# Writing the second layer's h into the place of its float16 halves

## The chip, the cores and the metric

One core of a Trainium2 chip runs the whole program. The metric is device time in microseconds (us) of one execution, measured before the change at a median of 731.52 us over three runs (729.27 to 731.77). One further execution was taken with the hardware profiler; that one took 728.16 us, and its trace spans 726.4 us from the first to the last instruction.

## The reference

The program is a top-k attention followed by two feed-forward layers. Everything is float32 in and out.

- Attention: 2 batches of 8 heads, 576 tokens, head size 64. Scores are q times k transposed over the root of 64; in each row only the 32 largest scores stay, then a softmax over them and the product with v.
- The result, as 1152 tokens by 512, goes through layer 1: `h = x @ w_in` (512 by 2048), `g = max(0.01 h, h)`, `g @ w_out` (2048 by 512).
- Then layer 2, with weights of its own: `h = x @ w_in`, `g = h * tanh(log(1 + exp(min(h, 20))))`, `g @ w_out`.

The change touches only how `g` of layer 2 is kept in memory while it is computed, and in what tile `g` of both layers lies.

## The kernel before, in words

The tokens are cut into nine tiles of 128 (t = 0 to 8). Attention runs in 72 slots, one per tile and head. Each feed-forward product keeps the accuracy of float32 by splitting both factors into a float16 "high" and a float16 "low" half and adding three float16 matmuls.

A feed-forward layer of a tile is four **steps**, one for each 512 of the 2048 columns of `h`. A step has two parts on TensorE:

- `product_in` (L634): 48 matmuls of 128x128 into one PSUM tile `ph`. `ph` has two places (pool `ps_m`), which it shares with other users of the tag "m".
- `product_out` (L648): 12 matmuls of 512 columns, which read the halves `gh` and `gl` of the step and add into `y` of the tile (`ps_y`, one place for both layers).

Between them the step makes `gh` and `gl` out of `ph`. In layer 1 that is `leaky` (L661): two ScalarE activations and one subtraction on GpSimd. In layer 2 it is `mish` (L669), a chain over four engines: ScalarE writes `hs` (the scaled h, L672) and `mc` (exp, L674) from `ph`; GpSimd clamps `mc` (L675); ScalarE squares, takes a logarithm and an exponential, all in place on `mc` (L676 to L678); VectorE multiplies by `hs` (L679); GpSimd makes `gh` and `gl` (L681, L682), for the last tile of layer 2 VectorE (`TF`, L820).

Memory is given out by tags, each with a fixed number of places; a new tile waits until the last reader of the place's former tile is done. Tag "t" (`TB = 3` places of 128x512 float32) serves `hs`, `mc`, the `lk` of `leaky`, and `o`, the output of a tile on its way to memory (L719). Tags "gh" and "gl" (`GB = 3` places each, 128x512 float16) serve the halves. They are asked for at the end of `mish` (L680), after its whole chain, and at the start of `leaky` (L663).

The function `step` (L797) emits the work: `first` of one step, that is `product_in` and the chain, and then, once more than `LAG = 3` steps are under way, `second`, that is `product_out`, of the step three before it. The layers alternate by tiles: four steps of layer 1 of tile t, then four of layer 2 of tile t-1; the last four are layer 2 of tile 8. During attention a slot emits one or two steps; after the last slot the rest of the steps follow by themselves.

Instructions are not issued in the order of the program. A planner simulates the engines when the kernel is built. It gives every instruction a priority (`at`, L837; a step gets one that is five slots later than its slot's attention) and, for each engine, picks the ready instruction of highest priority; an instruction that needs a place not yet free is not ready. What comes out is a fixed order for each engine, and on the chip each engine follows it and waits at semaphores.

Of the kernel before, what the change touches and what calls it, by code (L numbers as in the profile page):

```python
# [8 lines left out]
F16 = mybir.dt.float16  # L9
BF16 = mybir.dt.bfloat16  # L10
F32 = mybir.dt.float32
# [7 lines left out]
def topk_attention_moe_moe2_kernel(  # L19
# [18 lines left out]
    P = 128  # L38
# [25 lines left out]
    tmp = ctx.enter_context(tc.tile_pool(name="tmp", bufs=1))  # L64
    xtp = ctx.enter_context(tc.tile_pool(name="xtp", bufs=1))
    gp = ctx.enter_context(tc.tile_pool(name="gp", bufs=1))
# [589 lines left out]
    GB = 3  # L656

    def halves():
        return [gp.tile([P, 512], F16, tag=c, name=c, bufs=GB) for c in ("gh", "gl")]

    def leaky(ph, g, beside):  # L661
        t = tmp.tile([P, 512], F32, tag="t", name="lk", bufs=TB)
        gh, gl = halves()  # L663
        nc.scalar.activation(gh, ph, AF.Prelu, scale=fac[0][:, g:g + 1], alpha=0.01)
        nc.scalar.activation(t, ph, AF.Prelu, scale=fac[0][:, g:g + 1], alpha=0.01)  # L665
        beside.tensor_tensor(out=gl, in0=t, in1=gh, op=ALU.subtract)  # L666
        return gh, gl

    def mish(ph, g, iv, beside):  # L669

        hs = tmp.tile([P, 512], F32, tag="t", name="hs", bufs=TB)
        nc.scalar.activation(hs, ph, AF.Identity, scale=fac[1][:, g:g + 1])  # L672
        c = tmp.tile([P, 512], F32, tag="t", name="mc", bufs=TB)
        nc.scalar.activation(c, ph, AF.Exp, scale=iv[:, g:g + 1])  # L674
        nc.gpsimd.tensor_scalar(out=c, in0=c, scalar1=E20, scalar2=0.0, op0=ALU.min, op1=ALU.max)  # L675
        nc.scalar.activation(c, c, AF.Square, bias=1.0)  # L676
        nc.scalar.activation(c, c, AF.Ln, scale=0.5, bias=0.5)
        nc.scalar.activation(c, c, AF.Exp, scale=-1.0)  # L678
        nc.vector.scalar_tensor_tensor(out=c, in0=c, scalar=1.0, in1=hs, op0=ALU.subtract, op1=ALU.mult)  # L679
        gh, gl = halves()  # L680
        beside.tensor_scalar(out=gh, in0=c, scalar1=1.0, scalar2=0.0, op0=ALU.mult, op1=ALU.add)  # L681
        beside.tensor_tensor(out=gl, in0=c, in1=gh, op=ALU.subtract)  # L682
        return gh, gl
# [3 lines left out]
    class Layer:  # L687
# [11 lines left out]
        def first(self, g):  # L699
            ph = product_in(2 * self.l, self.hi, self.lo, g)  # L700
            beside = nc.vector if FG * self.t + g >= TF[self.l] else nc.gpsimd
            self.gs[g] = mish(ph, g, self.iv, beside) if self.l else leaky(ph, g, beside)
# [20 lines left out]
    TB = 3  # L723
# [138 lines left out]
    for i in range(-2, NS):  # L862
# [22 lines left out]
        if i >= 0:  # L885
            t, h = slots[i]
# [15 lines left out]
    n = NS  # L902
# [35 lines left out]
```

## Time and profile before

| | |
|---|---|
| median of three runs | 731.52 us (729.27 to 731.77) |
| the profiled execution | 728.16 us, its span 726.4 us |
| mean granted TensorE clock | 0.950 |
| TensorE busy | 636.1 us, 88% of the span |
| VectorE busy | 550.6 us, 76% |
| ScalarE busy | 547.7 us, 75% |
| GpSimd busy | 457.5 us, 63% |

Busy time is an average over a span with several stages: attention runs to about 617 us, the first `hs` is written at 267.9 us, and after 617 us only steps of the two layers are left. In the rows further down, PE is TensorE (PEld its weight loads), DVE VectorE, ACT ScalarE, POOL GpSimd, and SPq the queue that issues the DMAs. A row of a list of waits names the waiting instruction, what released it, then us in total, how many times, and the longest.

### The profile page before, as it was taken

Reading aid. Unit: us, or ns where it says so; the run is one execution under the profiler, and the core shown is the slowest. Engines: PE = TensorE matmul, PEld = TensorE weight load, DVE = VectorE, ACT = ScalarE, POOL = GpSimd, SP = SyncE. Lnnn points to the kernel's source line nnn. Section 1 sums busy time; section 2 is a strip of 40 time slices with the busy share of each in tenths; the row PEclk is TensorE's granted clock in tenths of the full one; section 3 lists DMA queues with packets and bytes.
Section 4 is the critical chain, followed back from the end, with each engine's and each line's share of the span. In section 5 each row is a group of like instructions: output and inputs, shape, how many; then the busy total and the mean of one; then the engine's idle time right before and its main releaser. Section 6 shows DMA issues by size and latency. Waiting matters only on the chain.

```text
span 726.4 us, 16854 instructions
## 1 busy us (share of the span) xinstructions
PE 636.1 (88%) x6420; PEld 455.5 (63%) x6420; DVE 550.6 (76%) x1199; ACT 547.7 (75%) x1068; POOL 457.5 (63%) x724
## 2 busy tenths in 40 slices
PE   2478788989977998889989999997999999999995
PEld 1254354557666886576667767666677777776772
DVE  3988988997899667798879899989799798120112
ACT  5497688988687888788979896877697788553643
POOL 2969967778965656566757676566567578333230
PEclk9999789998966997999999999999999999999999
DMA  8662373352332102243256223343444343200000
GB/s 290 229 220 84 116 272 121 108 176 75 124 116 74 60 1 54 61 83 74 39 111 113 51 56 72 65 82 61 65 78 71 74 60 55 62 17 16 1 16 29
DMA packets 107217, 64.14 MB, mean 88 GB/s; under 512 B 93696, under 2 KB 97792, under 8 KB 107136
## 3 DMA queue, kind: packets, MB, share of 16 engines
q1 hardware_dynamic: 107136, 63.06, 34.0%
q8 instruction: 50, 0.82, 0.5%
q14 instruction: 31, 0.25, 0.1%
HBM read 41.16 MB, written 2.36 MB: 60 GB/s over the span
## 4 chain that ended last, share of the span: by engine, by line
PE 34%; DVE 17%; ACT 16%; DMA 13%; POOL 13%; issue 7%; SPq 0%; POOLq 0%; ACTq 0%; DVEq 0%
DMA pts<-warena 6%; DVE top L512 6%; POOL warena L158 5%; PE ph L643 4%; PE ph L644 4%; PE ph L645 4%; DVE wk L515 4%; PE y L652 4%; PE y L654 4%; PE y L653 4%; DMA warena<-in_moe_w_in_dram 3%; PE lp L263 2%; ACT wk L537 2%; PE sps L497 2%; POOL warena L570 2%
## 5 line engine op out<-in xcount | busy, mean ns | idle before, releaser
L643 PE MATMUL ph<-xt,warena 128*128 128x128 f16 x1152 | 206.2, 222 | 3.1 <-ACT mc L674 2.4
L644 PE MATMUL ph<-xt,warena 128*128 128x128 f16 x1152 | 205.8, 222 | 0.0
L645 PE MATMUL ph<-xt,warena 128*128 128x128 f16 x1152 | 205.7, 222 | 0.0
L512 DVE MAX8 top<-wk 128x8 f32<-128x576 f32 x216 | 158.4, 751 | 1.2
L644 PEld LDWEIGHTS <-warena 128*128 128x128 f16 x1152 | 114.9, 100 | 8.2 <-issue 3.5
L643 PEld LDWEIGHTS <-warena 128*128 128x128 f16 x1152 | 115.0, 100 | 7.7 <-issue 2.2
L652 PE MATMUL y<-warena,gl 128*128 128x512 f16 x288 | 110.4, 383 | 6.9 <-ACT o L720 2.2
L645 PEld LDWEIGHTS <-warena 128*128 128x128 f16 x1152 | 114.5, 99 | 2.4 <-issue 1.0
L158 POOL TENSOR_TENSOR warena<-warena 128x256 int32<-128x256 int32 x128 | 104.2, 847 | 17.3 <-DVE warena L219 5.2
L654 PE MATMUL y<-warena,gh 128*128 128x512 f16 x288 | 110.2, 383 | 0.0
L653 PE MATMUL y<-warena,gh 128*128 128x512 f16 x288 | 110.0, 382 | 0.0
L515 DVE MATCH_REPLACE8 wk<-top,wk 128x576 f32<-128x576 f32 x144 | 106.9, 742 | 0.0
L537 ACT ACTIVATE wk<-sc,nb,iv 128x576 f32<-128x576 f32 x72 | 62.4, 867 | 20.7 <-POOL nb L530 20.4
L497 PE MATMUL sps<-kst,qst 128*128 128x288 f16 (+1 forms) x320 | 63.3, 306 | 9.7 <-ACT sc L499 7.4
L512 DVE MAX8 top<-sc 128x8 f32<-128x576 f32 x72 | 53.8, 747 | 21.4 <-ACT sc L499 17.7
L679 DVE SCALAR_TENSOR_TENSOR mc<-mc,hs 128x512 f32<-128x512 f32 x36 | 25.5, 708 | 55.3 <-ACT mc L678 55.3
L499 ACT COPY sc<-sps 128x288 f32<-128x288 f32 x144 | 53.7, 397 | 11.9 <-PE sps L497 11.8
L538 ACT ACTIVATE wk<-wk,nb 128x576 f32<-128x576 f32 x72 | 56.0, 777 | 8.5 <-POOL nb L534 7.6
L666 POOL TENSOR_TENSOR gl<-lk,gh 128x512 f16<-128x512 f32 x36 | 42.8, 1191 | 20.8 <-ACT lk L665 19.9
L530 POOL TENSOR_SCALAR nb<-top,iv 128x1 f32<-128x1 f32 x72 | 25.2, 350 | 47.0 <-DVE top L512 40.0
L263 PE MATMUL lp<-warena,diag 128*128 128x512 f32 x80 | 50.8, 722 | 3.1 <-POOL diag L258 1.8
L515 DVE MATCH_REPLACE8 wk<-top,sc 128x576 f32<-128x576 f32 x72 | 53.5, 743 | 0.0
(192 smaller groups left out, 1543.2 us busy)
## 6 DMA issues: line engine op xcount, KB each, us to landing
warena<-in_moe_w_in_dram SPq DMA_DIRECT2D x16, 1024.0 KB, 5.5
warena<-in_moe_w_out_dram SPq DMA_DIRECT2D x11, 1024.0 KB, 5.0
warena<-in_moe_w_out_dram SPq DMA_DIRECT2D x10, 512.0 KB, 3.3
out_dram<-o SPq DMA_DIRECT2D x9, 256.0 KB, 2.2
qr<-in_q_dram SPq DMA_DIRECT2D x8, 256.0 KB, 3.4
rawkv<-in_v_dram SPq DMA_DIRECT2D x8, 256.0 KB, 3.7
rawkr<-in_k_dram SPq DMA_DIRECT2D x6, 256.0 KB, 3.2
rawkv<-in_k_dram SPq DMA_DIRECT2D x2, 256.0 KB, 8.2
```

Source lines behind the costliest of these rows:

```text
L158: nc.gpsimd.tensor_tensor(out=o[:, a:a + PIECE], in0=o[:, a:a + PIECE], in1=x[:, a:a + PIECE], op=ALU.add)
L263: nc.tensor.matmul(lp, lhsT=diag, rhs=raws[c + i], start=True, stop=False)
L497: nc.tensor.matmul(sps[p0:p0 + n, :HS], lhsT=lq[:, c, p0:p0 + n], rhs=rk[:, half * HS:(half + 1) * HS], start=(c == 0), stop=(c == 1))
L512: queued(nc.vector.max(out=top[:, 8 * r:8 * r + 8], in_=src))
L515: queued(nc.vector.match_replace(out=wk, in_to_replace=top[:, 8 * r:8 * r + 8], in_values=src, imm_value=NEG))
L537: nc.scalar.activation(e, sc, AF.Prelu, bias=nb[:, 0:1], scale=iv, alpha=1e30)
L643: nc.tensor.matmul(o, lhsT=wb, rhs=xa, start=(c == 0), stop=False)
L644: nc.tensor.matmul(o, lhsT=wa, rhs=xb, start=False, stop=False)
L645: nc.tensor.matmul(o, lhsT=wa, rhs=xa, start=False, stop=(c == KC - 1))
L652: nc.tensor.matmul(y, lhsT=gb, rhs=whi(j), start=(g == 0 and f == 0), stop=False)
L653: nc.tensor.matmul(y, lhsT=ga, rhs=wlo(j), start=False, stop=False)
L654: nc.tensor.matmul(y, lhsT=ga, rhs=whi(j), start=False, stop=(g == FG - 1 and f == 3))
```

## The change

`gh` and `gl` become the two halves of one tile of 128x2x512 float16, tag "g", with three places. Together they take the same memory as before. In layer 1 nothing else changes. In layer 2 that tile is asked for at the start of `mish`, and `hs`, a 128x512 float32, is written over the whole of it. `hs` is read for the last time by the multiplication on VectorE, whose result goes to `mc`; after it `gh` and `gl` are written over `hs`. Tag "t" no longer holds `hs`.

```diff
     def halves():
-        return [gp.tile([P, 512], F16, tag=c, name=c, bufs=GB) for c in ("gh", "gl")]
+        return gp.tile([P, 2, 512], F16, tag="g", name="gg", bufs=GB)
 
     def leaky(ph, g, beside):
         t = tmp.tile([P, 512], F32, tag="t", name="lk", bufs=TB)
-        gh, gl = halves()
+        both = halves()
+        gh, gl = both[:, 0], both[:, 1]
...
     def mish(ph, g, iv, beside):
 
-        hs = tmp.tile([P, 512], F32, tag="t", name="hs", bufs=TB)
+        both = halves()
+        hs = both.rearrange("p c n -> p (c n)").bitcast(F32)
         nc.scalar.activation(hs, ph, AF.Identity, scale=fac[1][:, g:g + 1])
...
         nc.vector.scalar_tensor_tensor(out=c, in0=c, scalar=1.0, in1=hs, op0=ALU.subtract, op1=ALU.mult)
-        gh, gl = halves()
+        gh, gl = both[:, 0], both[:, 1]
         beside.tensor_scalar(out=gh, in0=c, scalar1=1.0, scalar2=0.0, op0=ALU.mult, op1=ALU.add)
         beside.tensor_tensor(out=gl, in0=c, in1=gh, op=ALU.subtract)
         return gh, gl
```

## Rows read from the trace of the kernel before

**Rows 1.** The page's first part: busy us, share of the span, instructions.
```profile
PE 636.1 (88%) x6420; PEld 455.5 (63%) x6420; DVE 550.6 (76%) x1199; ACT 547.7 (75%) x1068; POOL 457.5 (63%) x724
```
**Rows 2.** Busy time by stage: length, busy us by engine, clock, DMA.
```profile
268.00:290.00 22.00, 18.41 (x159) 15.05 (x157) 14.42 (x32) 20.20 (x49) 12.93 (x20) 0.77 0.19 44
...
310.00:600.00 290.00, 272.87 (x3279) 200.38 (x3278) 260.96 (x577) 236.77 (x494) 189.12 (x342) 0.99 0.39 72
600.00:690.70 90.70, 89.45 (x1045) 65.63 (x1043) 25.40 (x52) 51.17 (x88) 39.17 (x50) 1.00 0.15 29
...
694.50:708.00 13.50, 13.49 (x205) 11.94 (x204) 3.07 (x5) 6.92 (x12) 3.32 (x4) 1.00 0.01 2
708.00:720.10 12.10, 8.17 (x37) 3.41 (x37) 5.14 (x10) 6.30 (x10) 1.78 (x2) 1.00 0.06 22
```
**Rows 3.** What TensorE waited for from 268 to 600 us.
```profile
PE av L583 <- DMA pts<-warena: 9.0, 7, 1.9
...
PE ph L643 <- ACT mc L674: 2.4, 2, 1.4
```
**Rows 4.** What TensorE waited for from 600 us to the end.
```profile
PE y L652 <- ACT o L720: 2.2, 1, 2.2
PE y L652 <- DVE gl L682: 1.7, 1, 1.7
...
PE y L652 <- POOL gl L682: 1.2, 1, 1.2
```
**Rows 5.** What ScalarE waited for from 600 us to the end.
```profile
ACT gh L664 <- PE y L654: 17.8, 5, 4.6
```
**Rows 6.** Groups by line: ScalarE, 268 to 617 us (count, busy us, mean ns, idle before).
```profile
L672 ACT ACTIVATE hs<-ph,fac 128x512 f32<-128x512 f32 x24 | 16.4, 683 | 7.0 <-PE ph L645 6.2 <-POOL gl L682 0.8
```
**Rows 7.** Instructions in time: TensorE near the end (start, us, instruction, [idle before]).
```profile
679.99 0.38 PE L652 MATMUL y<-warena,gl 128*128 128x512 f16 x1
...
682.58 0.22 PE L643 MATMUL ph<-xt,warena 128*128 128x128 f16 x1
...
685.26 0.38 PE L652 MATMUL y<-warena,gl 128*128 128x512 f16 x1
...
691.92 0.39 PE L652 MATMUL y<-warena,gl 128*128 128x512 f16 x1 [1.18 <-POOL gl L682]
...
710.22 0.38 PE L652 MATMUL y<-warena,gl 128*128 128x512 f16 x1 [2.23 <-ACT o L720]
...
720.03 0.39 PE L652 MATMUL y<-warena,gl 128*128 128x512 f16 x1 [1.67 <-DVE gl L682]
```
**Rows 8.** Instructions in time: ScalarE in the attention stage.
```profile
425.98 0.69 ACT L672 ACTIVATE hs<-ph,fac 128x512 f32<-128x512 f32 x1 [0.61 <-PE ph L645]
...
433.58 0.67 ACT L674 ACTIVATE mc<-ph,iv 128x512 f32<-128x512 f32 x1
```
**Rows 9.** Instructions in time: ScalarE near the end.
```profile
680.19 0.69 ACT L672 ACTIVATE hs<-ph,fac 128x512 f32<-128x512 f32 x1 [2.35 <-PE ph L645]
...
683.26 0.69 ACT L674 ACTIVATE mc<-ph,iv 128x512 f32<-128x512 f32 x1
...
704.80 0.69 ACT L672 ACTIVATE hs<-ph,fac 128x512 f32<-128x512 f32 x1 [0.63 <-DVE gl L682]
...
709.48 0.69 ACT L720 ACTIVATE o<-y,ivo 128x512 f32<-128x512 f32 x1 [0.63 <-DVE gl L682]
...
712.28 0.69 ACT L672 ACTIVATE hs<-ph,fac 128x512 f32<-128x512 f32 x1 [0.94 <-DMA out_dram<-o]
...
714.32 0.69 ACT L674 ACTIVATE mc<-ph,iv 128x512 f32<-128x512 f32 x1 [0.83 <-DVE mc L679]
```
**Rows 10.** The tile xt from 689 us on, and its transposing DMA.
```profile
L621 SPq DMA_TRANSPOSE xt<-xp x1: 1232/1232/1232, 690.2 to 690.2; - x1
...
DMA to landing us min/median/max: 3.0/3.0/3.0
```
**Rows 11.** The tile hs: duration in ns (min/median/max), first and last start.
```profile
L679 DVE SCALAR_TENSOR_TENSOR mc<-mc,hs x36: 669/686/1141, 279.4 to 718.0; 128x512 f32<-128x512 f32 x36
```

## The prediction

> **What bounds the kernel now.** I read the page's busy times first: TensorE is the fullest engine at 88% [rows 1]. Then the busy time by stage, which says where the missing 12% lie: from 310 to 600 us TensorE is at 272.87 of 290 us (94%), from 600 to 690.7 at 99%, from 694.5 to 708 at all of it, and only between 708 and 720.1, before the last product, does it fall to 8.17 of 12.1 [rows 2]. So from 310 us on the program ends when TensorE has done its work, and what can be won is its idle time. Third, TensorE's list of waits: between 268 and 600 us most of what it waits for is attention's (9.0 us for the transposed weights `pts` alone), and 2.4 us, in two stalls, are a `product_in` that waits for exp (`mc`, L674) to have read the `ph` it wants to overwrite [rows 3]. After 600 us there are three stalls of layer 2: 2.2 us for `o`, 1.7 and 1.2 us for `gl` [rows 4]. These 7.5 us are what the change can reach.
>
> Why they arise is in ScalarE's order of time. The `hs` at 680.19 us is followed by its exp only at 683.26; near the end `hs` at 704.80, `o` at 709.48, `hs` at 712.28 and exp at 714.32 were each released by the last reader of a tile of tag "t" (VectorE's `gl`, again `gl`, the DMA of `o`, VectorE's multiplication) [rows 9]. With two of three "t" places to a chain, one and a half chains are under way at a time.
>
> **The change, part by part.**
>
> *Instructions.* None is added or taken away, and shapes, types and engines stay: cost 0. In `leaky` the first write is to `gh` as before, and its place comes free with the same `product_out`: 0.
>
> *The new wait.* A place of tag "g" is now held from `hs`, not from `gh`, on. `hs` of a step therefore waits for the `product_out` three steps earlier, which the program puts right behind the step's own `product_in`. One `product_in` takes 685.26 - 682.58 = 2.68 us and one `product_out` 682.58 - 679.99 = 2.59 us [rows 7], so `hs` starts some 2.6 us later in the last stage. Queued behind it on ScalarE are the exp of the same step and whatever attention has there; exp itself now needs only a "t" place and can go first. Waiting for its result is the `product_out` of three steps on, 3 x (2.68 + 2.59) = 15.8 us after the `product_in`. A chain from exp to the release of its `product_out` took 720.03 - 714.32 = 5.7 us for the last step [rows 7, 9], so with 2.6 us of wait and 0.7 us of `hs` it is ready after 9.0 us, 6.8 us early. `leaky` has this wait already: its `gh` waited five times for a `product_out`, up to 4.6 us [rows 5], and no stall of TensorE goes back to it [rows 4]. In attention 24 chains, so 48 steps of both layers, lie in 349 us [rows 6], 7.3 us a step against 5.27 alone; stretched alike, the `product_out` ahead of `hs` is 2.6 x 7.3 / 5.27 = 3.6 us, and `ph` is held for that and two activations of 0.7 us, about 5 us (an estimate). In the stalled case it was held from 425.98 to 434.25 us, 8.3 us [rows 8]. So I take 0; the upper end is the slower rival below.
>
> *The "t" places.* A chain takes one of three instead of two. Stall by stall:
>
> - The 1.18 us before 691.92 us [rows 7]. The chain in question is the one whose exp came 3.07 us behind its `hs` [rows 9]. With a place at hand its `gl` is ready before 690.74 and that `product_out` ends 1.18 us earlier. Next late is the transposed input of the last tile: its DMA is issued at 690.2 us and lands 3.0 us later, 693.2 [rows 10], before the end of that product. Between 0 and 1.18; I take 1.0, since the landing bounds it hardly.
> - The 2.23 us before 710.22. `y` has one place, so the last tile's first `product_out` waits until `o` has read it. `o` waited for a "t" place until 709.48 [rows 9]. Afterwards the three places hold one exp each and the oldest is done before this `y` is. Between 0.8 (two activations of 0.7 us ahead of `o` on ScalarE) and 2.23; I take 2.2.
> - The 1.67 us before 720.03. Without the stall above, the last `product_in` ends at 710.22 - 2.23 = 707.99 and three products of 8.14 / 3 = 2.71 us (710.22 to 718.36) follow, to 716.13. The last `hs` needs the place that the first of them frees, at 710.70. If ScalarE takes exp first, at 708.0, `hs` ends at 711.4 and `gl`, 2.0 us after the multiplication's start (718.0 to 720.03 [rows 7, 11]), at 713.4: the stall is gone. If `hs` goes first, exp starts at 711.3 and `gl` is there at 711.3 + 5.7 = 717.0, which leaves 0.9 us. So 0.8 to 1.67; I take 1.2, between the two orders.
> - The 2.4 us in attention [rows 3]: 0 to 2.4. I take 0.6, since the 9.0 us of waits for `pts` in the same stretch are ahead and behind in one fixed order and take most of what is freed.
>
> A rule of the Trainium skill speaks against the change. The trace shows the multiplication, which reads `mc` and `hs`, at a median of 686 ns with one at 1141 [rows 11]. "SBUF — State Buffer", section "Who interferes with whom", says that a VectorE instruction with two SBUF inputs contends with a GpSimd instruction that reads SBUF, so that one of the two is held. More chains at a time then mean more such meetings; by the trace's worst case, 0.45 us on the last chain, the sum would be 4.5 us instead of 5.0, by the median 5.0.
>
> The sum, made against the profiled execution: 1.0 + 2.2 + 1.2 + 0.6 = **5.0 us**, between 0 + 0.8 + 0.8 + 0 = 1.6 and 7.5. It goes from a span of 726.4 to 721.4 and from 728.16 to 723.2 us. That execution is 3.4 us under the median of 731.52; I carry the difference over: 731.52 - 5.0 = **726.5 us**. A measurement can hardly tell less than 0.5%, 3.7 us, from no change here.
>
> **The rivals.**
>
> - *Slower: the "g" places become the bound.* If the planner puts `hs` late behind attention's work, `ph` is held by `hs` as it is now by exp, and the next `product_in` but one stalls TensorE. Price: the two such stalls of before were 1.2 us each on average [rows 3]; at 8 of the 24 chains in attention [rows 6] that is 9.7 us, against 4.4 us won at the end: 731.5 - 4.4 + 9.7 = 736.8 us. It decides once `ph` is held over some 8 us at every third chain. For it: ScalarE is at 75% and its order is fixed ahead. Against it: the 5 us worked out above, and the rows of `leaky`. A new order in attention that lengthens the waits for `pts` would show in the same place, but would not name `hs`.
> - *No difference: the exp doesn't go ahead.* `hs` stands in front of exp in ScalarE's order, both wait for the `product_out`, and the places gained don't start a chain sooner. Then only `o` comes free (2.2 us), the last stall keeps 0.9 us, and the plan of attention is as good as before: -2.2 - 0.8 = -3.0, so 728.5 us; with attention's waits 1 or 2 us longer, 730. For it: in every pair of before `hs` precedes exp [rows 9].
> - *More: the clock.* From 268 to 290 us the granted clock was 0.77, TensorE moving between its two levels, 1.2 and 2.4 GHz, with 3.6 us of idle time [rows 2]. Here the first chains of layer 2 begin. If they come sooner and fill it, up to 22 x (1 - 0.77) = 5.1 us more are won: 721.4 us. Against it: what it did there was mostly attention's.
>
> **How the numbers follow.** The forecast, 726.5 us, has 0.42; the clock's case 0.08; no difference 0.30; slower 0.20. Faster by over 0.5% is the first two, 0.50; within 0.5% 0.30; slower 0.20. The range reaches down to 720.5, a microsecond below the clock's case, and up to 736, short of the slower rival's 736.8, which leaves out its upper half (0.10) and some 0.05 below. The forecast's own range is 724.0 (all 7.5 us) to 729.9 (1.6 us).
>
> **What would show it.** Right: exp directly behind its `hs` or ahead of it, `hs` released by a `product_out` (L654), `o` at once behind its `y`, no wait for `o` in TensorE's list after 600 us, and at most one for `gl`. Wrong: `product_in` waiting for `hs` (L672) in attention; longer waits for `pts`; the idle time of TensorE between 310 and 600 us above the 17 us of before; or attention ending later, so that TensorE has more left after it.

## The result and the profile after

The changed kernel is faster: against the kernel before, ratio 0.9855 (95% interval 0.9818 to 0.9892), medians 718.97 us (715.21 to 720.49, four runs) and 731.64 us. By the ratio that is 10.6 us on 731.5, where the forecast said 5.0. (The medians lie 12.7 us apart; the gains below go by the ratios.) The profiled execution took 718.89 us, with a span of 717.1 us, 9.3 us less than before.

Busy time by stage of the changed kernel, in stretches like those of [rows 2] (columns: stretch, length, TensorE busy, weight loads, VectorE, ScalarE, GpSimd, granted clock, DMA share, GB/s); the last two lines are two such stretches of the kernel before:

```profile
268.00:310.00 42.00, 35.81 (x249) 23.50 (x247) 24.42 (x59) 33.79 (x80) 22.64 (x33) 0.80 0.18 42
310.00:600.00 290.00, 280.09 (x3416) 208.07 (x3415) 266.84 (x597) 242.33 (x509) 193.28 (x351) 0.99 0.38 74
600.00:717.10 117.10, 111.29 (x1238) 79.20 (x1235) 28.36 (x59) 62.22 (x105) 41.00 (x54) 1.00 0.15 29
...
268.00:310.00 42.00, 35.15 (x304) 26.34 (x302) 29.31 (x71) 35.27 (x83) 23.85 (x38) 0.84 0.25 57
600.00:726.40 126.40, 116.43 (x1309) 83.18 (x1307) 33.61 (x66) 66.93 (x113) 46.04 (x58) 1.00 0.13 27
```

TensorE's idle time (length less busy) from 310 to 600 us fell from 17.1 us [rows 2] to 9.9. From 600 us to the end it fell from 10.0 us (126.4 less 116.4 in the trace before) to 5.8. Those are 7.2 and 4.2 us. Between 268 and 310 us it is 6.2 against 6.9. Ahead of 268 us it is 58.7 against 56.3; the order of the instructions there is the same, so this is scatter between executions. Over the whole span idle fell by 9.6 us, and busy time (636.5) is what it was (636.1 [rows 1]).

TensorE's list of waits from 268 to 600 us, which answers to [rows 3]:

```profile
PE av L583 <- DMA pts<-warena: 2.5, 4, 1.0
...
PE xt L627 <- DVE u L100: 1.3, 2, 1.0
...
PE y L652 <- POOL gg L684: 1.0, 1, 1.0
```

The 9.0 us for `pts` are 2.5 (how much of that is scatter comes up below), and `product_in` no longer waits for exp. The list from 600 us to the end, which answers to [rows 4] (`gg` is the joined tile; VectorE and GpSimd write `gl` at L684):

```profile
PE y L652 <- POOL gg L684: 1.3, 1, 1.3
PE y L652 <- DVE gg L684: 0.9, 1, 0.9
```

The wait for `o` is gone. The two for `gl` are still there, one shorter. ScalarE's list of the same stretch shows the new wait, `hs` (L674) behind a `product_out`, beside that of `leaky` (L665) [rows 5]:

```profile
ACT gg L674 <- PE y L654: 13.0, 10, 2.3
ACT gg L665 <- PE y L654: 12.0, 5, 4.1
```

And the group of the 24 chains in attention, which answers to [rows 6], now with exp (L676) beside it:

```profile
L674 ACT ACTIVATE gg<-ph,fac 128x512 f32<-128x512 f32 x24 | 16.5, 687 | 6.7 <-PE y L654 6.5
L676 ACT ACTIVATE mc<-ph,iv 128x512 f32<-128x512 f32 x24 | 16.5, 686 | 0.0
```

Exp waits for nothing there: it stands right behind its `hs`. Over the 24 chains exp started 4.5 us after its `hs` before, 0.6 us after it now; over the 12 of the last stage 2.0 and 0.6 us (means of the starts in the timelines).

### The profile page after: what moved, and what is told of

Same layout as the page of the kernel before. It is cut to its first block, busy times and chain, and to the rows that moved or that the text cites. A ratio compares the mean times of both kernels' runs of the same rounds, so it can differ in the third digit from the quotient of the medians.

```text
span 717.1 us, 16836 instructions
## 1 busy us (share of the span) xinstructions
PE 636.5 (89%) x6420; PEld 455.2 (63%) x6420; DVE 546.3 (76%) x1199; ACT 544.9 (76%) x1068; POOL 455.4 (64%) x724
## 4 chain that ended last, share of the span: by engine, by line
PE 47%; DVE 16%; ACT 11%; DMA 10%; POOL 9%; issue 5%; SPq 1%; POOLq 0%; ACTq 0%; DVEq 0%
PE ph L645 6%; PE y L653 6%; PE y L652 6%; PE ph L643 6%; PE y L654 6%; PE ph L644 6%; DVE top L512 5%; DVE wk L515 3%; POOL warena L158 3%; PE sps L497 3%; DMA warena<-in_moe_w_in_dram 3%; DMA warena<-in_moe_w_out_dram 3%; DMA pts<-warena 2%; DVE warena L222 1%; ACT warena L260 1%
## 5 line engine op out<-in xcount | busy, mean ns | idle before, releaser
L643 PE MATMUL ph<-xt,warena 128*128 128x128 f16 x1152 | 202.9, 220 | 1.4 <-ACT xt L628 1.0
L644 PE MATMUL ph<-xt,warena 128*128 128x128 f16 x1152 | 202.9, 220 | 1.1 <-DVE u L100 1.1
L645 PE MATMUL ph<-xt,warena 128*128 128x128 f16 x1152 | 202.9, 220 | 0.0
L158 POOL TENSOR_TENSOR warena<-warena 128x256 int32<-128x256 int32 x128 | 105.9, 860 | 18.3 <-DVE warena L219 6.3
L652 PE MATMUL y<-warena,gg 128*128 128x512 f16 x288 | 111.3, 386 | 5.0 <-POOL gg L684 2.3
L653 PE MATMUL y<-warena,gg 128*128 128x512 f16 x288 | 111.4, 387 | 0.0
L654 PE MATMUL y<-warena,gg 128*128 128x512 f16 x288 | 111.3, 387 | 0.0
L537 ACT ACTIVATE wk<-sc,nb,iv 128x576 f32<-128x576 f32 x72 | 62.7, 871 | 32.4 <-POOL nb L530 32.2
L681 DVE SCALAR_TENSOR_TENSOR mc<-mc,gg 128x512 f32<-128x512 f32 x36 | 26.1, 724 | 50.5 <-ACT mc L680 50.5
L538 ACT ACTIVATE wk<-wk,nb 128x576 f32<-128x576 f32 x72 | 56.3, 782 | 4.7 <-POOL nb L534 3.9
L667 POOL TENSOR_TENSOR gg<-lk,gg 128x512 f16<-128x512 f32 x36 | 42.9, 1191 | 23.5 <-ACT lk L666 23.2
L570 POOL TENSOR_TENSOR warena<-wk,warena 128x512 f16<-128x512 f32 x32 | 37.6, 1174 | 26.0 <-ACT warena L569 25.5
```

The source lines that it names most:

```text
L158: nc.gpsimd.tensor_tensor(out=o[:, a:a + PIECE], in0=o[:, a:a + PIECE], in1=x[:, a:a + PIECE], op=ALU.add)
L537: nc.scalar.activation(e, sc, AF.Prelu, bias=nb[:, 0:1], scale=iv, alpha=1e30)
L538: nc.scalar.activation(e, e, AF.Exp, bias=nb[:, 2:3], accum_out=self.sums[:, h:h + 1])
L643: nc.tensor.matmul(o, lhsT=wb, rhs=xa, start=(c == 0), stop=False)
L644: nc.tensor.matmul(o, lhsT=wa, rhs=xb, start=False, stop=False)
L645: nc.tensor.matmul(o, lhsT=wa, rhs=xa, start=False, stop=(c == KC - 1))
```

## The experiments

All ratios are to the kernel before on the same chip. Joining the two halves alone changes nothing: in `e1_tail` below they are joined for all tiles while `hs` stays in tag "t" up to tile 5, and up to 627 us the order on every engine is that of the kernel before, instruction for instruction. So all of the effect comes from where `hs` stands.

**1. The two stages apart.** Do the 10.6 us come from one stage or from two? `e1_tail` applies the change from tile 6 on; `e2_attn`, with `t < 6` in the same place, up to tile 5:

```diff
-        both = halves()
-        hs = both.rearrange("p c n -> p (c n)").bitcast(F32)
+        if t >= 6:
+            both = halves()
+            hs = both.rearrange("p c n -> p (c n)").bitcast(F32)
+        else:
+            hs = tmp.tile([P, 512], F32, tag="t", name="hs", bufs=TB)
...
+        if not (t >= 6):
+            both = halves()
```

> h is written into the halves' place only for tiles 6 to 8 of layer 2, the last twelve chains, after attention; up to there every engine's order is that of the kernel before. If the gain is the sum of two stages (my theory), only the last stage's is here: TensorE idle after 600 us falls from 10.0 us to about 6, idle from 310 to 600 us stays at 17, and the time falls by 4 us, to about 727.5. If the whole gain hung on one stage, the rival, the time would be 721 (the last stage alone) or 731 (attention alone).

> h is written into the halves' place only for tiles 0 to 5 of layer 2, the 24 chains during attention; up to the first chain of tile 6 every engine's order is that of the changed kernel. Sum of two stages: TensorE idle from 310 to 600 us is about 10 us as in the changed kernel, idle after 600 us is about 10 us as before with the wait for o back at some 2 us, and the time falls by 6 to 7 us, to about 725. One stage alone: 721 or 731.

Measured: `e1_tail` 0.9953 (0.9929 to 0.9977), 3.4 us; `e2_attn` 0.9929 (0.9904 to 0.9955), 5.2 us. Together 8.6 of the 10.6 us, within their intervals. Idle time of TensorE from 310 to 600 us: 15.0 us in the first, 10.5 in the second; after 600 us 7.0 and 8.8. So there are two gains; by the medians and the idle times the larger is in attention, though the two intervals overlap, and its 5.2 us are less than the 6 to 7 I expected. `e1_tail` also shows the scatter: up to 627 us its order is that of the kernel before, and yet it has 15.0 us of idle time there and not 17.1. The list of waits after 600 us of `e2_attn` has the three stalls of [rows 4] back:

```profile
PE y L652 <- ACT o L727: 2.2, 1, 2.2
PE y L652 <- DVE gg L689: 1.7, 1, 1.7
PE y L652 <- POOL gg L689: 1.2, 1, 1.2
```

**2. Places or the luck of a new order?** The planner lays out all that follows anew when one thing changes, and the waits for `pts` that shrank have nothing to do with layer 2's places. `b_lswap` is a re-plan without any new place, a mild one: on TensorE the new order starts only at 326 us, not from the first steps on as the expectation has it, and in the traces a matmul moves by 5 places on average, against 19 by the change.

```diff
+        nc.scalar.activation(t, ph, AF.Prelu, scale=fac[0][:, g:g + 1], alpha=0.01)
         nc.scalar.activation(gh, ph, AF.Prelu, scale=fac[0][:, g:g + 1], alpha=0.01)
-        nc.scalar.activation(t, ph, AF.Prelu, scale=fac[0][:, g:g + 1], alpha=0.01)
```

> The kernel before, with the two activations of layer 1's leaky written in the other order; no place and no instruction changes, but the planner's order differs on all engines from the first steps on. If the gain in attention comes from the free places (theory), a new order by itself doesn't give it: TensorE idle from 310 to 600 us stays at 15 to 19 us and the time within 728 to 735. If it was the luck of a new order (rival), the idle time lands anywhere from 8 to 25 us and the time from 722 to 740.

Measured: 1.0008 (0.9986 to 1.003), idle 15.4 us. `a_lswap` is the same edit in the changed kernel:

> The changed kernel with the two activations of leaky written in the other order: a new order on all engines, no other places. Theory (the gain belongs to the places): idle from 310 to 600 us 8 to 12 us, ratio 0.982 to 0.991. Rival (luck of an order): idle 8 to 25 us, ratio 0.975 to 1.01.

Measured: 0.9867 (0.9841 to 0.9893), idle 10.8 us. The gain goes with the change. The two orders without it are nearly the same, so this alone would not rule out luck; the later runs add six more orders, all with a gain.

**3. The swap that was meant as a second re-plan.** `b_swap` is the kernel before with exp written ahead of `hs`:

```diff
         hs = tmp.tile([P, 512], F32, tag="t", name="hs", bufs=TB)
-        nc.scalar.activation(hs, ph, AF.Identity, scale=fac[1][:, g:g + 1])
         c = tmp.tile([P, 512], F32, tag="t", name="mc", bufs=TB)
         nc.scalar.activation(c, ph, AF.Exp, scale=iv[:, g:g + 1])
+        nc.scalar.activation(hs, ph, AF.Identity, scale=fac[1][:, g:g + 1])
```

> The kernel before, with exp written ahead of hs in the chain of layer 2; same places and instructions, a new order from the first chain of layer 2 on. Theory: idle from 310 to 600 us stays at 15 to 19 us, the time within 728 to 735. Rival (luck of a new order): idle 8 to 25 us, time 722 to 740, independent of the other swap's.

Measured: 0.9772 (0.9722 to 0.9823), faster than the changed kernel by its median (the intervals just touch), with idle 9.9 us. Both sides of my expectation missed the time: it is no mere re-plan. A chain still takes the same two places, but exp now takes the first and runs through its powers while `hs`, read only by the multiplication, waits: exp starts 2.7 us ahead of `hs` on average in attention. In ScalarE's list of waits from 268 to 610 us, before (first line) it is exp that waits for a place, which the multiplication frees; in `b_swap` (second line) it is `hs`, and exp waits for its `ph` alone:

```profile
ACT mc L674 <- DVE mc L679: 1.4, 2, 1.2
...
ACT hs L674 <- DVE mc L679: 1.2, 1, 1.2
```

TensorE's list of waits of `b_swap` after 600 us has one row left:

```profile
PE y L652 <- ACT o L720: 0.5, 1, 0.5
```

To see whether that was luck, `b_swap_lswap` adds the edit of 2 to it:

> The kernel before with exp ahead of hs and also leaky's activations in the other order. Alone the first gave 0.977 and the second 1.001. If exp ahead of hs is the cause, 0.972 to 0.985 and idle from 310 to 600 us 8 to 12 us; if the first was a lucky order, 0.985 to 1.005 and idle 12 to 20 us.

Measured: 0.9779 (0.9747 to 0.9811), idle 8.8 us, clear of the changed kernel's interval. Not luck, though this order too is near that of `b_swap` (4 places on average).

**4. Is it the third place?** `a_tb2` is the changed kernel with `TB = 2`.

> The changed kernel with two places of tag t instead of three. Rival (the number of places held by chains makes the gain): two places for exp, lk and o together are fewer than a chain and a half needs, exp is late again, TensorE idle from 310 to 600 us returns to 15 us or more, the wait for o returns, ratio 0.995 to 1.01. Theory (what counts is that exp doesn't stand behind an hs that already holds a place): exp stays within 1.5 us of hs on average, the idle time stays at 8 to 12 us, ratio 0.983 to 0.992, with at most the stall for o back at the end.

Measured: 0.9893 (0.9855 to 0.993). Exp starts 1.1 us after `hs`; idle 12.4 us from 310 to 600 us, a little over what I expected, and 5.8 after 600, and no wait for `o`. So two places for exp, `lk` and `o` give nearly the whole gain that three do. By itself this leaves open that a chain now takes one place of two, not two of three; but `b_swap` has the old three places, two to a chain, and gains as well. What held the kernel before was not how many places there were, but that an `hs` with nothing to do yet took one ahead of the exp that starts the chain.

**5. Both at once.** `a_swap` is the changed kernel with the edit of `b_swap`.

> The changed kernel with exp ahead of hs, so that exp doesn't stand behind an hs that waits for a product_out. Theory: the last stage's idle time falls from 5.8 us to under 4.5 (the last stall of 0.9 us goes, the one before it shrinks), idle from 310 to 600 us stays at 8 to 12 us, ratio 0.975 to 0.984, as good as the other kernel with exp first. If the wait for product_out cost nothing (rival), the ratio is that of the changed kernel, 0.983 to 0.99.

Measured: 0.9898 (0.9851 to 0.9945). The last stage did what was expected (idle 4.1 us, no stall for `gl`), but attention did not: idle 13.2 us, and among its waits 2.2 us for `gl`. My expectation for the ratio failed; the two edits don't add. The rival's range has the ratio, but not its reason: in the last stage the wait for `product_out` did cost something.

**6. Why exp first beats the changed kernel.** Idle time over the whole span is 81.0 us in `b_swap` and 80.6 in the changed kernel, so the 4.9 us between their spans (712.2 and 717.1) lie in TensorE's busy time, 631.2 against 636.5, for the same 6420 matmuls. Of these 5.3 us, 2.0 lie ahead of the matmul at which the two orders part (263.7 and 264.4 us) and are scatter; from there on it is 427.5 against 430.8. The stage whose clock differs most is that of the first four chains. `h1_first_swap` takes `b_swap`'s way for tile 0 and the changed kernel's for the rest, `h2_first_after`, with `t == 0` for `t > 0`, the reverse:

```diff
-        both = halves()
-        hs = both.rearrange("p c n -> p (c n)").bitcast(F32)
-        nc.scalar.activation(hs, ph, AF.Identity, scale=fac[1][:, g:g + 1])
+        if t > 0:
+            both = halves()
+            hs = both.rearrange("p c n -> p (c n)").bitcast(F32)
+            nc.scalar.activation(hs, ph, AF.Identity, scale=fac[1][:, g:g + 1])
         c = tmp.tile([P, 512], F32, tag="t", name="mc", bufs=TB)
         nc.scalar.activation(c, ph, AF.Exp, scale=iv[:, g:g + 1])
+        if not (t > 0):
+            hs = tmp.tile([P, 512], F32, tag="t", name="hs", bufs=TB)
+            nc.scalar.activation(hs, ph, AF.Identity, scale=fac[1][:, g:g + 1])
...
+        if not (t > 0):
+            both = halves()
```

> Exp ahead of hs, with hs in tag t, for tile 0 of layer 2 alone (the first four chains, 268 to about 310 us); all later tiles as in the changed kernel. Theory: exp first beat the changed kernel by what TensorE's clock lost in that first stretch (its idle time is the same, 81 us both); the granted clock from 268 to 310 us is above 0.88, TensorE idle from 310 to 600 us 8 to 13 us and after 600 us about 6 us, ratio 0.975 to 0.983. Rival: exp first wins in all of attention because its hs doesn't hold a place of the halves; then this one is near the changed kernel, 0.984 to 0.99.

> The other way round: tile 0 of layer 2 as in the changed kernel, exp ahead of hs with hs in tag t from tile 1 on. Theory: granted clock from 268 to 310 us about 0.80 as in the changed kernel, idle after 600 us about 4 us, ratio 0.982 to 0.988. Rival: the later tiles make the difference, ratio 0.973 to 0.980 whatever the clock of the first stretch.

Measured: 0.9809 (0.9769 to 0.9848) and 0.9866 (0.9822 to 0.9909), both ratios inside the theory's range, though the interval of the first reaches into its rival's. The stretch from 268 to 310 us, first of `b_swap`, then of `h1_first_swap`, then of `h2_first_after`:

```profile
268.00:310.00 42.00, 34.91 (x275) 22.63 (x274) 30.34 (x73) 35.88 (x85) 23.90 (x37) 0.92 0.21 48
```

```profile
268.00:310.00 42.00, 35.78 (x274) 22.88 (x272) 30.39 (x73) 35.88 (x85) 23.93 (x37) 0.88 0.21 48
```

```profile
268.00:310.00 42.00, 35.67 (x248) 23.23 (x246) 24.50 (x61) 33.90 (x79) 22.64 (x33) 0.80 0.18 42
```

With exp first in those four chains the clock is 0.88 to 0.92 and 274 or 275 matmuls go through in 35 to 36 us; the other way 0.80 and 248. TensorE's busy time from the matmul at which the orders part is 427.4 us in `h1_first_swap` and 426.8 in `b_swap_lswap`, and 430.8 to 433.0 in the four traces with the changed kernel's order there (changed, `e2_attn`, `a_lswap`, `h2_first_after`). So the changed kernel gives back some 3 us. Exp first alone doesn't bring them: `a_swap`, with exp first but `hs` in the halves' place, has 0.89 in this stretch with only 247 matmuls, then 0.97 from 310 to 600 us, and 432.0 us of busy time. The intervals of the two mixed kernels overlap a little, so the sign rests on the medians (714.33 and 719.03 us) and on the clock together.

The idle times side by side (us of TensorE; exp less hs is the mean of 24 chains):

| kernel | exp less hs | idle 310 to 600 | idle after 600 | ratio |
|---|---|---|---|---|
| before | 4.5 | 17.1 | 10.0 | 1 |
| b_lswap | 4.1 | 15.4 | 8.7 | 1.001 |
| e1_tail | 4.4 | 15.0 | 7.0 | 0.995 |
| e2_attn | 0.6 | 10.5 | 8.8 | 0.993 |
| changed | 0.6 | 9.9 | 5.8 | 0.986 |
| a_lswap | 0.6 | 10.8 | 5.8 | 0.987 |
| a_tb2 | 1.1 | 12.4 | 5.8 | 0.989 |
| a_swap | -3.2 | 13.2 | 4.1 | 0.990 |
| h2_first_after | -1.8 | 11.9 | 4.7 | 0.987 |
| h1_first_swap | -0.3 | 10.3 | 5.8 | 0.981 |
| b_swap | -2.7 | 9.9 | 4.0 | 0.977 |
| b_swap_lswap | -3.0 | 8.8 | 4.1 | 0.978 |

The three with exp over 4 us behind `hs` have 15.0 to 17.1 us of idle time in attention, the nine others 8.8 to 13.2. Part of that is scatter (before and `e1_tail` have one order there, and so have changed and `e2_attn`), but the two groups stay apart. `b_swap` and `b_swap_lswap` beat both kernels; exp first, with `hs` left in tag "t", is the better edit.

## Why the prediction was right, and where it was off

**Direction and mechanism: right.** Exp stands right behind `hs`, `hs` is released by a `product_out`, no stall of TensorE names `hs`, and `o` follows its `y` by 1.2 us, in time for the next tile. One sign failed: two waits for `gl` are left, where the prediction allowed one. All of the gain is idle time of TensorE, as the first paragraph of the prediction had it.

**The sum: too small by half, and the time in the range partly by luck.** 10.6 us lie outside the 1.6 to 7.5 us of the forecast's own terms. The time is inside the whole range because that reached down for the clock's case, which did not happen here.

**The new wait, costed at 0: nearly.** `hs` waited ten times for a `product_out` in the last stage, 13.0 us in all, and idle time fell there all the same. But exp stands behind that `hs`. In `a_swap`, where it doesn't, the stage has 4.1 us of idle time and not 5.8, so the wait costs up to 1.7 us; 0.9 of it the prediction had put into its last term.

**The 1.18 us before 691.92: wrong, 1.0 taken, nothing won.** The stall is 1.28 us now. What was late was not the DMA but the chain itself, on VectorE and GpSimd:

```profile
680.44 0.63 ACT L680 ACTIVATE mc<-mc 128x512 f32<-128x512 f32 x1
...
682.12 0.16 DVE L100 TENSOR_SCALAR u<-tot 128x1 int32<-128x1 int32 x1 [5.98 <-PE tot L119]
682.20 0.69 DVE L681 SCALAR_TENSOR_TENSOR mc<-mc,gg 128x512 f32<-128x512 f32 x1
...
683.05 0.62 POOL L683 TENSOR_SCALAR gg<-mc 128x512 f16<-128x512 f32 x1 [3.12 <-DVE x1i L105]
683.75 0.61 POOL L677 TENSOR_SCALAR mc<-mc 128x512 f32<-128x512 f32 x1
684.44 1.48 POOL L684 TENSOR_TENSOR gg<-mc,gg 128x512 f16<-128x512 f32 x1
...
685.97 0.39 PE L652 MATMUL y<-warena,gg 128*128 128x512 f16 x1 [1.28 <-POOL gg L684]
```

These are lines of the timelines of ScalarE, VectorE, GpSimd and, the last, TensorE. The multiplication (L681) had its operand at 681.07 us, but VectorE's order has the first instruction of the next input (L100) ahead of it, and that one waited for TensorE's `tot`: 1.1 us. The kernel before has the same delay to a lesser degree (operand at 688.04, multiplication at 688.80), so tag "t" was not all that held this chain, as the prediction took it to be. In `a_swap` and `b_swap` the multiplication stands ahead of L100, and this stall is gone.

Then the next chain, free to start, puts its clamp (L677) between `gh` and `gl` of the one that TensorE waits for, and that `gl` took 1.48 us where the median of the group is 1.16. It ran beside VectorE's work on the next input (L620, 0.99 us at 683.91), which reads two operands in memory. In the twelve traces all 59 of the subtractions that make `gl` (L667 and L684 here) that took over 1.25 us ran beside a `scalar_tensor_tensor` of VectorE, the form of L620; others that did so stayed under that. The rule that the prediction weighed ("SBUF — State Buffer", "Who interferes with whom", in the Trainium skill) is of such meetings. The trace agrees in kind, and the 0.32 us of this `gl` are of the size of the 0.45 us worked out there. The multiplication itself went from 669/686/1141 ns [rows 11] to

```profile
L681 DVE SCALAR_TENSOR_TENSOR mc<-mc,gg x36: 668/692/1255, 283.7 to 708.6; 128x512 f32<-128x512 f32 x36
```

**The 2.23 us for `o`: right,** gone in the changed kernel and back in `e2_attn`.

**The 1.67 us at the end: 0.8 to 1.67 with 1.2 taken; 0.74 won.** Of the two orders that the prediction worked out, the planner took `hs` first, for which it gave 0.9 us left; 0.93 is left:

```profile
704.67 0.69 ACT L674 ACTIVATE gg<-ph,fac 128x512 f32<-128x512 f32 x1 [1.00 <-PE y L654]
705.26 0.68 ACT L676 ACTIVATE mc<-ph,iv 128x512 f32<-128x512 f32 x1
...
710.75 0.38 PE L652 MATMUL y<-warena,gg 128*128 128x512 f16 x1 [0.93 <-DVE gg L684]
```

So the three terms of the last stage made 2.9 us instead of 4.4; a wait of 1.2 us for attention's weights at 608 us, which I had not counted, went too, and the stage gave 4.2 us in all.

**Attention: the term that failed in size, 0.6 taken between 0 and 2.4; 7.2 measured in the profile, 5.2 by `e2_attn`.** The step that failed is the bound: I took the stalls that name layer 2 (2.4 us) for all that could be won, and argued that the waits for `pts` would swallow most of it. The 2.4 us went whole: from 310 to 600 us `product_in` waits for exp for 2.2 to 2.4 us in the three traces with exp late, and in none of the nine others. And the idle time fell by more than that. Where the rest of it lies is only in part settled. The waits for `pts` fell from 9.0 to 2.5 us; but `e1_tail`, in the very order of before, has 5.5 us of them (first line), and `a_lswap`, with the whole gain, 5.6 (second line):

```profile
PE av L583 <- DMA pts<-warena: 5.5, 5, 2.1
...
PE av L583 <- DMA pts<-warena: 5.6, 7, 1.6
```

So up to 3.5 of those 6.5 us can be scatter between executions. A wait is entered under what ended last, not under why TensorE had nothing else in front of it. In TensorE's order of instructions, ahead of the same matmul of attention (the 49th, 97th, 145th and 193rd of L583), so many `product_in` stand:

| matmul of L583 | 49 | 97 | 145 | 193 |
|---|---|---|---|---|
| before | 21.8 | 27.0 | 37.0 | 50.2 |
| b_lswap | 22.0 | 26.7 | 37.0 | 49.6 |
| changed | 23.2 | 28.0 | 39.2 | 50.0 |
| a_tb2 | 23.9 | 28.0 | 39.2 | 50.0 |
| b_swap | 22.9 | 28.0 | 39.2 | 49.8 |
| a_lswap | 22.1 | 27.2 | 38.4 | 49.5 |

In three of the four kernels where exp isn't late, one to two steps more lie ahead of the first three, and TensorE has them to do while a DMA lands. Ahead of the fourth there are no more, and `a_lswap`, which keeps the gain, has hardly more ahead of the first two. In the trace attention itself then runs later for most of the way, the weights' activation (L537) of the 45th slot at 446.4 us instead of 432.8, and still its last one is earlier, 609.8 against 613.9 us. That chains which start sooner give the planner steps to put there may be part of the gain; the table does not show it, and an order with the steps ahead and exp late was not tried. Shown is that the gain comes with the early exp; the way it takes to the rest of the idle time stays open.

**The clock's case: not in this change.** It asked for more than before's 0.84 in the first stretch; the changed kernel has 0.80. In `b_swap`, with 0.92, it is there in kind: from the matmul at which the orders part TensorE's busy time is 427.5 us, against 428.6 to 430.1 in before, `b_lswap` and `e1_tail`, whose TensorE orders are alike there. That is 1.1 to 2.6 us, about half at most of the 5.1 us that the prediction gave it; from 310 to 600 us `b_swap` has 0.98 where before has 0.99.

**The slower rival** did not happen: `ph` of the 24 chains was held, from the end of its `product_in` to the end of the second activation that reads it, for 5.6 us on average, near the 5 us worked out against it. Its threshold was wrong, though: before, 11 of the 24 were held for 8 us or more, with only two stalls. **The rival of no difference** had the right order, `hs` ahead of exp and behind the `product_out`, and drew the wrong end from it: what mattered was that exp was no longer 4.5 us behind.

## What to carry to other kernels

When a chain takes two places of a pool, look at which it takes first: a value needed only at the end, written first, can hold the place that the next chain's first instruction wants. Writing the start of the chain first cost no memory here and gave more than the new place did. Where a planner fills one engine with the work of a second stream, read what that stream can gain as idle time of the filled engine over the stage, not only from the stalls that name the stream. And before you split that idle time by what ended each wait, look at a second trace of the same order: here one order had 17.1 and 15.0 us of idle time, and 9.0 and 5.5 us of one wait. A re-plan without the resource tells a gain from the luck of the order only as far as it really moves the order.

## What the runs showed of the hardware

In the stretch from 268 to 310 us the granted clock (levels 2.4 and 1.2 GHz) went with TensorE's order of instructions and repeated with it: 0.84, 0.88 and 0.86 with the order of the kernel before (before, `e1_tail`, `b_lswap`), 0.80, 0.80, 0.84 and 0.80 with that of the changed kernel (changed, `e2_attn`, `a_lswap`, `h2_first_after`), and 0.92, 0.88 and 0.92 with exp first and `hs` in tag "t" (`b_swap`, `h1_first_swap`, `b_swap_lswap`); the first and the third group touch. TensorE was idle for 6.1 to 8.0 us of the 42 in all ten. `a_tb2` and `a_swap`, each with an order of its own, had 0.76 and 0.89. So the idle time of a stage does not tell its clock, and one trace tells it to some 0.04.
